# Whole x in two buffers, the multiple of 2 pi on another engine, joins in two pieces: one change in the Theta stage of a fused network

## The chip, the cores and the metric

The kernel runs on one core of a Trainium2 chip. The metric is the device time of one execution in microseconds; lower is better. The engines are TensorE (PE, matrix products), VectorE (DVE), ScalarE (ACT), GpSimd (POOL) and SyncE (SP), whose queue issues most of the DMA transfers.

## The reference, cut to what matters

Three blocks follow each other: an attention with sigmoid weights, a gated unit with a mixing over the sequence, and a block with phases. B is 4, the sequence 448, the width 768. The change lies in the third block:

```python
theta = x @ w_theta
zr, zi = x * np.cos(theta), x * np.sin(theta)
y = np.einsum('ts,bsd->btd', w_tok_r, zr) + np.einsum('ts,bsd->btd', w_tok_i, zi)
u = x + y
return u + np.maximum(u @ w_ch, 0.0)
```

## The kernel before

Every product in fp32 is made of three products of split operands: a high part (`acopy` on ScalarE, rounded to the matrix engine's format) and a low part (`sub` on VectorE, the rest), multiplied as high by high, high by low and low by high. The operand x lies in DRAM as `x_d[b]`, 768 by 448, feature by token.

**The Theta stage** works in units `(b, h, i)`: batch b, one half h of 384 features, one block i of 128 tokens. Blocks 0 to 2 are whole; the last 64 tokens of two batches make one block together, i = 3 of the even batch, so that there are 14 blocks (the list `steps`) and 28 units. `theta(b, h, i)` makes 18 matmuls of 384 columns (lines 636 to 638) into one of two PSUM banks `pt`, and then reduces the angle: line 641 forms round(theta / 2 pi) by adding and taking off (line 642) a large constant `MAGIC`; lines 643 and 644 take off the multiple of 2 pi in two parts; line 645 clamps. Line 643 is the last that reads the bank. ScalarE then forms Abs, Sin and the cosine as a Sin (lines 647 to 649), VectorE multiplies both by x^T (line 626), and `split` makes the two operands z of the token product. `tok(b, h, i, Z)` adds a unit's 18 matmuls of 448 columns (9 for a tail block) into six banks `py`, and at i = 3 VectorE adds x (line 59 through `add`) and y goes to DRAM. A list `queue` holds three units: `tok` of a unit is written down three units behind its `theta`.

**x is needed in three forms.** As the stationary operand `XT` of Theta, in blocks: `load_x2` loads a block `xf` from `x_d` (384 KB) and splits it, three blocks ahead. As x^T, token by feature, for the multiplications: `halve` transposes `x_d` by DMA as 16-bit halves into `halved`, `part_planes` sorts the two planes of a block by DMA into `xp`, and `join_planes` puts them together into `xr` with one ScalarE instruction of 1536 16-bit elements in each partition. And as the whole x for the addition at the end of a batch: `load_x` into the single buffer `xb`.

**Order.** In this stage only SP's queue keeps the order in which the program is written; the order of the other engines is laid out by a planner at build time, from the order of the program and from its own costs and due times, and each engine then works through its list in order. From batch 1 on `sums_ch` prepares blocks of w_ch alongside. Ahead of Theta lie the projections of the last batches (`project`, `ppo`); behind it the channel products of the last stage, whose first operands come from y in DRAM (`load_y`, `first_operands`).

Of the kernel before, what the change touches and what calls it, by code (L numbers as in the profile page):

```python
# [10 lines left out]
F32 = mybir.dt.float32  # L11
F32R = mybir.dt.float32r
# [10 lines left out]
P = 128  # L23
# [27 lines left out]
def net(ctx: ExitStack, tc: tile.TileContext, kq, vd, vl, w_in, w_sp, bsp, w_out, w_th, w_tok, w_ch, out):  # L51
# [3 lines left out]
    def sub(o, a, b):  # L55
        ve.tensor_tensor(out=o, in0=a, in1=b, op=ALU.subtract)  # L56
# [4 lines left out]
    def acopy(o, a, f=AF.Copy):  # L61
        se.activation(o, a, f)  # L62
# [416 lines left out]
    def halve(b):  # L479

        halved[b] = pxa.tile([P, 7, DM], U16, tag="xa", name="xa")
        nc.sync.dma_start_transpose(halved[b], x_d[b].bitcast(U16))
# [60 lines left out]
    es_a.close()  # L543


    pxb = es_w.enter_context(tc.tile_pool(name="pxb", bufs=1, reuse_waits="tile"))
    es_b = ExitStack()
    pb = es_b.enter_context(tc.tile_pool(name="pb", bufs=2, reuse_waits="tile"))
    pb.tile([P, LINE // 2], F32, name="gap2", bufs=1)
    XT, XR = {}, {}  # L550

    def load_x2(b, i):

        xf = pb.tile([P, KC, 2, LT], F32, tag="xf", name="xf")
        src = xf.rearrange("p c b t -> p c (b t)")
        if i < 3:
            nc.sync.dma_start(src, x_d[b][:, i * P:(i + 1) * P].rearrange("(c p) t -> p c t", p=P))
        else:
            for n in range(2):
                nc.sync.dma_start(xf[:, :, n, :], x_d[b + n][:, L0:S].rearrange("(c p) t -> p c t", p=P))  # L560
        t = pb.tile([P, KC, 2, P], F32R, tag="XT", name="XT", bufs=3)
        if not XT:
            pb.tile([P, LINE // 2], F32, name="gap3", bufs=1)
        acopy(t[:, :, 0, :], src)
        sub(t[:, :, 1, :], src, t[:, :, 0, :])
        XT[b, i] = t

    planes = {}
# [1 line left out]
    def part_planes(b, i):  # L570

        tail = i == 3
        n = b - b % 2 if tail else b
        if (n, i) not in planes:
            planes[n, i] = pb.tile([P, 2, DM], U16, tag="xp", name="xp")
        for j in (b % 2,) if tail else range(2):
            src = halved[b][:, 6 if tail else 2 * i + j, :]
            for h in range(2):
                nc.sync.dma_start(planes[n, i][halves[j], h, :], src[h:P:2, :])

    def join_planes(b, i):

        t = pb.tile([P, DM], F32, tag="xr", name="xr")
        acopy(t.bitcast(U16).rearrange("p (d h) -> p h d", h=2), planes[b, i])
        XR[b, i] = t

    def whole(pool, tag):
# [2 lines left out]
    def load_x(b):  # L590
        t = X2[b] = whole(pxb, "xb")
        nc.sync.dma_start(t, x_d[b].rearrange("(c p) t -> p c t", p=P))

    X2 = {}
    steps = [(b, i) for b in range(B) for i in range(4 - b % 2)]
    for n in steps[:2]:
        load_x2(*n)
        part_planes(*n)
    load_x2(*steps[2])
    join_planes(*steps[0])  # L600
    part_planes(*steps[2])
    se.activation(warm, XR[steps[0]][:, 0:4], AF.Sin, scale=0.0)
    for b, g in ((B - 2, G), (B - 1, Gn)):
        for d in range(KC):
# [23 lines left out]
    def theta(b, h, i):  # L628
        if (b, h, i) in LEFT:
            return [LEFT.pop((b, h, i))]  # L630
        hs = slice(h * HALF, (h + 1) * HALF)
        ps = ps_t.tile([P, 512], F32, tag="t", name="pt")
        o = ps[:, :HALF]
        t = XT[b, i]
        for k in range(KC):
            te.matmul(o, t[:, k, 0, :], thh[:, k, hs], start=k == 0, stop=False)  # L636
            te.matmul(o, t[:, k, 0, :], thl[:, k, hs], start=False, stop=False)  # L637
            te.matmul(o, t[:, k, 1, :], thh[:, k, hs], start=False, stop=k == KC - 1)  # L638
        r = pm.tile([P, HALF], F32, tag="r", name="r")
        m = pm.tile([P, HALF], F32, tag="m", name="m")  # L640
        ve.tensor_scalar(out=m, in0=o, scalar1=INV2PI, scalar2=MAGIC, op0=ALU.mult, op1=ALU.add)  # L641
        ve.tensor_scalar_sub(m, m, MAGIC)
        ve.scalar_tensor_tensor(out=r, in0=m, scalar=-C1, in1=o, op0=ALU.mult, op1=ALU.add)  # L643
        ve.scalar_tensor_tensor(out=r, in0=m, scalar=-C2, in1=r, op0=ALU.mult, op1=ALU.add)
        ve.tensor_scalar(out=r, in0=r, scalar1=PIN, scalar2=-PIN, op0=ALU.min, op1=ALU.max)  # L645
        x = XR[b, i][:, hs]
        se.activation(m, r, AF.Abs)  # L647
        se.activation(r, r, AF.Sin)
        se.activation(m, m, AF.Sin, bias=hpi, scale=-1.0)
        if i < 3:  # L650
            mul(m, x, m)
            mul(r, x, r)
            return [split(m, "zr"), split(r, "zi")]
        for n, a in enumerate((slice(0, 64), slice(64, P))):
            g = pz.tile([P, HALF], F32, tag="th", name="th", bufs=1)
            mul(g[0:64], x[a], m[a])
            mul(g[64:P], x[a], r[a])
            z = pz.tile([P, 2, HALF], F32R, tag="zl", name="zl", bufs=4)
            acopy(z[:, 0, :], g)
            sub(z[:, 1, :], g, z[:, 0, :])  # L660
            LEFT[b + n, h, i] = z
        return [LEFT.pop((b, h, i))]
# [5 lines left out]
    def tok(b, h, i, Z):  # L668
        if i == 0:
            for d in range(3):  # L670
                acc[h, d] = ps_y.tile([P, 512], F32, tag="y", name=f"py{d}")
        for d in range(3):
            ds = slice(d * P, (d + 1) * P)
            o = acc[h, d][:, :S]
            for n, z in enumerate(Z):
                c = 6 if i == 3 else 3 * n + i
                te.matmul(o, z[:, 0, ds], tkh[:, c, :], start=i == 0 and n == 0, stop=False)
                te.matmul(o, z[:, 0, ds], tkl[:, c, :], start=False, stop=False)
                te.matmul(o, z[:, 1, ds], tkh[:, c, :], start=False, stop=i == 3)
        if i == 3:  # L680
            for d in range(3):
                dc = 3 * h + d
                r = pz.tile([P, S], F32, tag="y", name="y", bufs=3)
                add(r, acc[h, d][:, :S], X2[b][:, dc, :])
                nc.sync.dma_start(y_d[b][dc * P:(dc + 1) * P, :], r)
# [41 lines left out]
    def sums_ch(n):  # L727

        if n % 3 == 0:
            c, s = quads[n // 3]  # L730
            q = pz.tile([P, 4, C2H], F32, tag="wq", name="wq", bufs=1)
            nc.sync.dma_start(q.rearrange("p (j i) f -> p j i f", j=2),
                              f_ch.rearrange("p (j c) (i f) -> p c j i f", j=2, i=2)[:, c, :, :, s])
            quad[:] = [q, c, s]
            return
        q, c, s = quad
        a11, a21, a12, a22 = (q[:, k] for k in range(4))
        if n % 3 == 1:
            for x, m in ((a11, "A11"), (a12, "A12")):
                half_part(x, m, c, s)  # L740
            for o, x, y, f in ((a22, a21, a22, ALU.add), (a21, a11, a21, ALU.subtract),
                               (a11, a22, a11, ALU.subtract), (a12, a12, a11, ALU.subtract)):
                nc.gpsimd.tensor_tensor(out=o, in0=x, in1=y, op=f)
        else:
            for x, m in ((a11, "S2"), (a22, "S1")):
                half_part(x, m, c, s)
            nc.sync.dma_start(f_s[:, c, :, s], q[:, 1:3])

    queue, done = [], []

    def unit(b, h, i):
        queue.append((b, h, i, theta(b, h, i)))
        if len(queue) > 3:
            tok(*queue.pop(0))
        if b >= CH_FROM and i < 3:
            sums_ch(len(done))
            done.append((b, h, i))

    with tc.manual_schedule(engines={mybir.EngineType.SP}):
        for b in range(B):  # L760
            for i in range(4):
                for h in range(2):
                    unit(b, h, i)
                    k = steps.index((b, i)) if (b, i) in steps else len(steps)
                    if h == 0:
                        if i == 1 and b % 2 == 0:
                            halve(b + 1)
                            part_planes(b + 1, 3)
                        if (b, i) == (1, 0):
                            halve(b + 1)  # L770
                        for n in steps[k + 1:k + 2]:
                            join_planes(*n)
                        for n in steps[k + 3:k + 4]:
                            part_planes(*n)
                        if i == 2:
                            load_x(b)
                    else:
                        for n in steps[k + 3:k + 4]:
                            load_x2(*n)
                        if (b, i) == (B - 1, 1):  # L780
                            Yf = {0: load_y(0, pxa)}
    es_m.close()
    es_th.close()
    py, p_t, p_y1 = (es_t.enter_context(tc.tile_pool(name=n, bufs=1, side="right", reuse_waits="tile"))
# [156 lines left out]
```

## Time and profile before

| | us |
|---|---|
| median of 3 runs (630.6 to 631.47) | 631.02 |
| the profiled execution | 629.19 |
| its span, first to last instruction | 627.4 |
| TensorE busy in it | 613.5 |
| VectorE busy | 426.4 |
| ScalarE busy | 334.7 |

The granted clock of TensorE was at its full level over the whole span. Times inside the execution count from the first instruction. A matmul's row shows its start and a modelled end; the rows of neighbours overlap, so what matters is the distance of their starts and the idle time in brackets, with the instruction that ended it.

### The profile page before, as it was taken

What the parts mean: (1) busy time and instruction counts of PE and PEld (TensorE: products, weight loads), DVE (VectorE), ACT (ScalarE), POOL (GpSimd) and SP (SyncE); (2) the same over time, 40 slices, a digit from 0 to 9 for tenths busy, and PEclk for the clock granted to TensorE, in tenths of its full rate; (3) what the DMA queues carried; (4) which work ended last, traced back from release to release, by engine and by line L of the source; (5) the groups of instructions that cost most, each with busy time, mean ns of one, the idle gap of its engine ahead of it and who ended that gap; (6) DMA issues with size and microseconds to landing.
All of it is one profiled execution on the core that took longest, in us unless ns stands there. A gap on an engine that the chain in (4) does not pass through costs nothing.

```text
span 627.4 us, 9178 instructions
## 1 busy us (share of the span) xinstructions
PE 613.5 (98%) x3296; PEld 506.9 (81%) x3296; DVE 426.4 (68%) x824; ACT 334.7 (53%) x544; POOL 24.3 (4%) x42
## 2 busy tenths in 40 slices
PE   7999999999999999999999999989999999999997
PEld 3456667756776689999999999979999989889896
DVE  3899566526754568884141677787797889679875
ACT  5798556553656335364264375455466466352540
POOL 0000000000001000100000000101001101000000
PEclk9999999999999999999999999999999999999999
DMA  8787588748864685865776416546368226344603
GB/s 319 244 272 208 194 270 261 254 155 287 284 210 152 183 280 193 256 207 177 193 217 174 105 50 217 111 152 201 100 153 245 70 91 225 115 167 132 242 31 133
DMA packets 95220, 118.13 MB, mean 188 GB/s; under 512 B 31171, under 2 KB 81733, under 8 KB 95173
## 3 DMA queue, kind: packets, MB, share of 16 engines
q1 hardware_dynamic: 87364, 104.69, 53.9%
q10 hardware_dynamic: 7808, 12.85, 5.6%
q8 instruction: 26, 0.43, 0.3%
q14 instruction: 22, 0.17, 0.1%
HBM read 73.57 MB, written 32.93 MB: 170 GB/s over the span
## 4 chain that ended last, share of the span: by engine, by line
PE 68%; DVE 17%; DMA 6%; ACT 6%; issue 2%; SPq 0%; ACTq 0%
PE psa L224 7%; PE pss L199 6%; PE psd L65 3%; PE psd L243 3%; DMA xf<-x_d 3%; PE ppo L66 3%; PE ppo L65 3%; PE ppo L67 3%; PE psd L67 3%; PE psd L66 3%; PE psd L244 3%; PE psd L245 3%; PE psp L450 2%; PE psp L449 2%; PE psp L451 2%
## 5 line engine op out<-in xcount | busy, mean ns | idle before, releaser
L186 ACT ACTIVATE af<-pss,bias 128x896 f32<-128x896 f32 x72 | 66.1, 1020 | 2.8 <-PE pss L199 2.8
L636 PE MATMUL pt<-thh,XT 128*128 128x384 f32 x168 | 57.2, 340 | 4.2 <-DVE r L643 4.2
L637 PE MATMUL pt<-thl,XT 128*128 128x384 f32 x168 | 56.8, 338 | 0.0
L224 PE MATMUL psa<-af,vr 128*64 128x448 f32 x288 | 56.8, 543 | 0.0
L638 PE MATMUL pt<-thh,XT 128*128 128x384 f32 x168 | 56.8, 338 | 0.0
L224 PEld LDWEIGHTS psa<-af,vr 128*64 128x64 f32 x288 | 19.6, 137 | 36.3 <-issue 35.4
L111 DVE SCALAR_TENSOR_TENSOR wq<-wraw,wq 128x384 int32<-128x384 int32 (+2 forms) x51 | 28.7, 594 | 24.1 <-ACT wraw L106 23.9
L62 ACT ACTIVATE ev<-psd 128x448 f32<-128x448 f32 (+1 forms) x30 | 17.0, 568 | 52.5 <-PE psd L67 23.2
L647 ACT ACTIVATE m<-r 128x384 f32<-128x384 f32 x28 | 14.6, 520 | 43.7 <-DVE r L645 43.7
L636 PEld LDWEIGHTS pt<-thh,XT 128*128 128x128 f32 x168 | 31.5, 188 | 5.9 <-DVE r L643 5.5
L65 PE MATMUL psd<-X,wih 128*128 128x448 f32 x96 | 35.6, 371 | 0.0
L106 ACT ACTIVATE wraw<-wraw 128x384 f32<-128x384 f32 (+2 forms) x51 | 29.7, 605 | 10.5 <-DVE wq L99 6.7
L66 PE MATMUL ppo<-g,wbh 128*128 128x448 f32 x96 | 35.2, 366 | 0.0
L65 PE MATMUL ppo<-g,wbh 128*128 128x448 f32 x96 | 35.1, 366 | 0.0
L67 PE MATMUL ppo<-g,wbl 128*128 128x448 f32 x96 | 35.1, 366 | 0.0
L67 PE MATMUL psd<-X,wil 128*128 128x448 f32 x96 | 35.1, 365 | 0.0
L66 PE MATMUL psd<-X,wih 128*128 128x448 f32 x96 | 35.1, 365 | 0.0
L56 DVE TENSOR_TENSOR X<-psa,X 128x448 fp32r<-128x448 f32 x24 | 15.0, 624 | 27.9 <-ACT X L62 27.9
L637 PEld LDWEIGHTS pt<-thl,XT 128*128 128x128 f32 x168 | 31.6, 188 | 0.4
L101 DVE SCALAR_TENSOR_TENSOR wq<-wraw,wq 128x384 int32<-128x384 int32 (+2 forms) x51 | 30.6, 600 | 1.8
L638 PEld LDWEIGHTS pt<-thh,XT 128*128 128x128 f32 x168 | 31.5, 188 | 0.0
L641 DVE TENSOR_SCALAR m<-pt 128x384 f32<-128x384 f32 x28 | 15.4, 551 | 19.6 <-DMA x_d<-x 17.9
(287 smaller groups left out, 1596.3 us busy)
## 6 DMA issues: line engine op xcount, KB each, us to landing
kqr<-in_kq SPq DMA_DIRECT2D x24, 448.0 KB, 4.8
wraw<-in_w_in SPq DMA_DIRECT2D x12, 512.0 KB, 5.6
x_d<-x ACTq DMA_DIRECT2D x24, 224.0 KB, 3.2
xp<-xa SPq DMA_DIRECT2D x56, 96.0 KB, 2.5
xb<-x_d SPq DMA_DIRECT2D x4, 1344.0 KB, 6.5
y_d<-y SPq DMA_DIRECT2D x24, 224.0 KB, 2.0
out_t<-o SPq DMA_DIRECT2D x24, 224.0 KB, 2.0
vr<-in_vd SPq DMA_DIRECT2D x24, 192.0 KB, 3.8
```

Source lines behind the costliest of these rows:

```text
L65: te.matmul(ps, wh, xh, start=first, stop=False)
L66: te.matmul(ps, wh, xl, start=False, stop=False)
L67: te.matmul(ps, wl, xh, start=False, stop=last)
L101: ve.scalar_tensor_tensor(out=self.q, in0=self.hi, scalar=-(2 ** 31), in1=self.q, op0=ALU.bitwise_and, op1=ALU.bitwise_or)
L106: se.activation(self.lo.bitcast(F32), self.hi.bitcast(F32), AF.Copy, scale=2.0 ** -112)
L111: ve.scalar_tensor_tensor(out=self.q, in0=self.lo, scalar=3, in1=self.q, op0=ALU.logical_shift_left, op1=ALU.bitwise_or)
L186: se.activation(af, ps[:, :, :S], AF.Sigmoid, bias=bias, scale=1.0 / math.sqrt(D))
L199: te.matmul(ps[:, j, :S], t[w][a, 0, c], t[x][a, 1, :], start=n == 0, stop=n == 2)
L224: te.matmul(ps[a, :S], t["v"][:, 2 * c + j, :], t["a"][c][:, j, :], start=False, stop=c == 2)
L636: te.matmul(o, t[:, k, 0, :], thh[:, k, hs], start=k == 0, stop=False)
L637: te.matmul(o, t[:, k, 0, :], thl[:, k, hs], start=False, stop=False)
L638: te.matmul(o, t[:, k, 1, :], thh[:, k, hs], start=False, stop=k == KC - 1)
```

## The change

Five things, in the code below. The blocks `xf` and `load_x2` go: `split_x` takes a block's high and low part out of the whole x in `X2[b]`, for which there are now two buffers, and `load_x` is called earlier (batch 0 before the stage, batch 1 in the first unit, batches 2 and 3 at block 1 of the batch ahead of them, behind the `tok` there). `XT` has two buffers in place of three and is split one block ahead. Line 641 becomes a ScalarE activation of the same arithmetic, and `r` and `m` have three buffers. `join_planes` makes two instructions of 768 elements. The calls in the loop over units stand in another order: splits, plane transfers and transposes ahead of a unit's `tok`, loads, joins and `sums_ch` behind it.

```diff
-    pxb = es_w.enter_context(tc.tile_pool(name="pxb", bufs=1, reuse_waits="tile"))
+    pxb = es_w.enter_context(tc.tile_pool(name="pxb", bufs=2, reuse_waits="tile"))
...
-    def load_x2(b, i):
-
-        xf = pb.tile([P, KC, 2, LT], F32, tag="xf", name="xf")
-        src = xf.rearrange("p c b t -> p c (b t)")
-        if i < 3:
-            nc.sync.dma_start(src, x_d[b][:, i * P:(i + 1) * P].rearrange("(c p) t -> p c t", p=P))
-        else:
-            for n in range(2):
-                nc.sync.dma_start(xf[:, :, n, :], x_d[b + n][:, L0:S].rearrange("(c p) t -> p c t", p=P))
-        t = pb.tile([P, KC, 2, P], F32R, tag="XT", name="XT", bufs=3)
+    def split_x(b, i):
+
+        t = pb.tile([P, KC, 2, P], F32R, tag="XT", name="XT")
...
-        acopy(t[:, :, 0, :], src)
-        sub(t[:, :, 1, :], src, t[:, :, 0, :])
+        if i < 3:
+            src = X2[b][:, :, i * P:(i + 1) * P]
+            acopy(t[:, :, 0, :], src)
+            sub(t[:, :, 1, :], src, t[:, :, 0, :])
+        else:
+            for n, a in enumerate(halves):
+                src = X2[b + n][:, :, L0:S]
+                acopy(t[:, :, 0, a], src)
+                sub(t[:, :, 1, a], src, t[:, :, 0, a])
         XT[b, i] = t
...
-        acopy(t.bitcast(U16).rearrange("p (d h) -> p h d", h=2), planes[b, i])
+        o = t.bitcast(U16).rearrange("p (d h) -> p h d", h=2)
+        for s in (slice(0, HALF), slice(HALF, DM)):
+            acopy(o[:, :, s], planes[b, i][:, :, s])
...
+    load_x(0)
     for n in steps[:2]:
-        load_x2(*n)
         part_planes(*n)
-    load_x2(*steps[2])
+    split_x(*steps[0])
     join_planes(*steps[0])
-    part_planes(*steps[2])
...
-        r = pm.tile([P, HALF], F32, tag="r", name="r")
-        m = pm.tile([P, HALF], F32, tag="m", name="m")
-        ve.tensor_scalar(out=m, in0=o, scalar1=INV2PI, scalar2=MAGIC, op0=ALU.mult, op1=ALU.add)
+        r = pm.tile([P, HALF], F32, tag="r", name="r", bufs=3)
+        m = pm.tile([P, HALF], F32, tag="m", name="m", bufs=3)
+        se.activation(m, o, AF.Copy, bias=MAGIC, scale=INV2PI)
...
-                    unit(b, h, i)
+                    z = theta(b, h, i)
                     k = steps.index((b, i)) if (b, i) in steps else len(steps)
                     if h == 0:
-                        if i == 1 and b % 2 == 0:
-                            halve(b + 1)
+                        for n in steps[k + 1:k + 2]:
+                            split_x(*n)
+                        for n in steps[k + 2:k + 3]:
+                            part_planes(*n)
+                    if (b % 2, i, h) in ((0, 1, 0), (1, 0, 1)) and b + 1 < B:
+                        halve(b + 1)
+                    queue.append((b, h, i, z))
+                    if len(queue) > 3:
+                        tok(*queue.pop(0))
+                    if h == 0:
+                        if (b, i) == (0, 0) or 0 < b < B - 1 and i == 1:
+                            load_x(b + 1)
+                    else:
+                        if b % 2 == 0 and i == 1:
                             part_planes(b + 1, 3)
-                        if (b, i) == (1, 0):
-                            halve(b + 1)
                         for n in steps[k + 1:k + 2]:
                             join_planes(*n)
-                        for n in steps[k + 3:k + 4]:
-                            part_planes(*n)
-                        if i == 2:
-                            load_x(b)
-                    else:
-                        for n in steps[k + 3:k + 4]:
-                            load_x2(*n)
-                        if (b, i) == (B - 1, 1):
-                            Yf = {0: load_y(0, pxa)}
+                    if b >= CH_FROM and i < 3:
+                        sums_ch(len(done))
+                        done.append((b, h, i))
+                    if (b, h, i) == (B - 1, 1, 1):
+                        Yf = {0: load_y(0, pxa)}
```

## Rows read from the trace of the kernel before

**Rows 1.** The page: busy time, share of the span and instructions of each engine.

```profile
PE 613.5 (98%) x3296; PEld 506.9 (81%) x3296; DVE 426.4 (68%) x824; ACT 334.7 (53%) x544; POOL 24.3 (4%) x42
```

**Rows 2.** Busy time in stretches of the Theta stage, TensorE, weight load, VectorE, ScalarE, GpSimd.

```profile
402.60:417.50 14.90, 12.30 (x65) 11.16 (x63) 11.67 (x26) 8.22 (x15) 1.18 (x2) 1.00 0.39 131
...
496.70:508.40 11.70, 10.15 (x55) 9.50 (x53) 9.10 (x20) 5.79 (x10) 0.00 (x0) 1.00 0.05 19
...
sum 197.50, PE 193.28 PEld 182.86 DVE 155.29 ACT 108.86 POOL 16.40; mean PE 38.66 PEld 36.57 DVE 31.06 ACT 21.77 POOL 3.28
```

**Rows 3.** Timeline of TensorE: start, duration, line, operands, [idle before, and what ended it].

```profile
402.58 0.34 PE L636 MATMUL pt<-thh,XT 128*128 128x384 f32 x1
...
408.04 0.44 PE L636 MATMUL pt<-thh,XT 128*128 128x384 f32 x1 [0.28 <-DVE r L643]
...
417.46 0.44 PE L636 MATMUL pt<-thh,XT 128*128 128x384 f32 x1 [2.32 <-DVE r L643]
...
476.10 0.34 PE L636 MATMUL pt<-thh,XT 128*128 128x384 f32 x1
...
508.41 0.44 PE L636 MATMUL pt<-thh,XT 128*128 128x384 f32 x1 [1.56 <-DVE r L643]
...
551.39 0.68 PE L833 MATMUL pb__5486<-Y,wch 128*128 128x448 f32 x2 [1.45 <-DVE y L59]
```

**Rows 4.** Timeline of VectorE.

```profile
400.70 0.55 DVE L643 SCALAR_TENSOR_TENSOR r<-m,pt 128x384 f32<-128x384 f32 x1
...
415.98 0.96 DVE L56 TENSOR_TENSOR XT<-xf,XT 128x768 fp32r<-128x768 f32 x1 [1.50 <-ACT XT L62]
...
504.66 0.56 DVE L626 TENSOR_TENSOR r<-xr,r 128x384 f32<-128x384 f32 x1 [2.07 <-ACT r L648]
...
543.24 1.70 DVE L56 TENSOR_TENSOR T<-yf,xa 128x448 f32<-128x448 f32 x3 [5.01 <-DMA yf<-y_d]
```

**Rows 5.** The chain of waits, 400 to 418 us: start, duration, what.

```profile
409.92 5.10 DMA xf<-x_d
...
415.10 0.85 ACT XT L62
...
416.85 0.56 DVE r L643
```

**Rows 6.** Timeline of ScalarE.

```profile
330.46 1.19 ACT L62 ACTIVATE g<-gf 128x448 fp32r<-128x448 f32 x2
...
502.32 1.94 ACT L62 ACTIVATE xr<-xp 128x1536 uint16<-128x1536 uint16 x1
```

**Rows 7.** VectorE's groups, 347 to 544 us: busy us, mean ns | idle before.

```profile
L641 DVE TENSOR_SCALAR m<-pt 128x384 f32<-128x384 f32 x28 | 15.4, 551 | 19.6 <-DMA x_d<-x 17.9 <-PE pt L638 1.7
...
L56 DVE TENSOR_TENSOR XT<-xf,XT 128x768 fp32r<-128x768 f32 x11 | 10.9, 992 | 8.5 <-ACT XT L62 8.5
```

**Rows 8.** ScalarE's groups, 347 to 544 us.

```profile
L62 ACT ACTIVATE xr<-xp 128x1536 uint16<-128x1536 uint16 x12 | 23.4, 1947 | 0.3 <-issue 0.3
...
L62 ACT ACTIVATE XT<-xf 128x768 fp32r<-128x768 f32 x11 | 9.2, 839 | 8.5 <-DMA xf<-x_d 8.5
```

**Rows 9.** Loads into xb: issues with KB and median landing; landing of all.

```profile
xb<-x_d SPq DMA_DIRECT2D x4, 1344.0 KB, 6.5
...
DMA to landing us min/median/max: 4.4/6.5/9.4
```

**Rows 10.** Timeline of SP's queue, the waits at its instructions included in their time.

```profile
317.64 0.39 SPq L557 DMA_DIRECT2D xf<-x_d  x1
...
456.22 5.41 SPq L685 DMA_DIRECT2D y_d<-y  x3
```

**Rows 11.** ScalarE's groups, 300 to 347 us: the eviction of a PSUM bank.

```profile
L62 ACT ACTIVATE x<-ppo 128x448 f32<-128x448 f32 x17 | 9.1, 540 | 13.8 <-PE ppo L67 8.3 <-PE psp L453 2.2 <-DMA x_d<-x 1.9
```

**Rows 12.** Waits of ScalarE, 347 to 544 us: us in total, times, longest.

```profile
ACT m L647 <- DVE r L645: 43.7, 20, 4.9
```

**Rows 13.** Waits of TensorE's weight load, whole span.

```profile
PEld pt L636 <- DVE r L643: 5.5, 4, 2.7
```

More of the change, by code (lines that the diff above doesn't have):

```diff
@@ L749, in net @@
     queue, done = [], []
[L751 to L757, printed above, removed]
     with tc.manual_schedule(engines={mybir.EngineType.SP}):
```

## The prediction, made before the change was run

> **What bounds the kernel.** I read the page first: TensorE is busy for 613.5 of 627.4 us [rows 1]. At most 13.9 us can come from anything but fewer matmuls, and the change removes no matmul. So the question is only where TensorE stands still, and whether the change touches those places. The busy time by stretches shows it for the Theta stage (346.8 to 544.3 us): 193.28 of 197.50 us, and the 4.2 us that are missing lie almost wholly in two short stretches, 2.60 us between 402.6 and 417.5 and 1.55 us between 496.7 and 508.4 [rows 2]. TensorE's own timeline then gives the three instructions that waited: 0.28, 2.32 and 1.56 us, together 4.16 us, each the first matmul of a Theta unit (L636), each released by L643 on VectorE [rows 3]. L643 is the last reader of a Theta bank in PSUM; there are two banks, so unit n+2 cannot begin before L643 of unit n has ended. Both places are where a batch ends: the token products of a tail block are 9 matmuls instead of 18, so Theta units follow each other faster, and six additions of x fall on VectorE there as well.
>
> Elsewhere the release is in time. Of the 26 hand-overs of a bank, four had no margin: these three and one more, where only the weight load waited [rows 13]. The closest of the other 22 is the one before unit 11: L643 starts at 400.70 and takes 0.55, the matmul comes at 402.58, so 1.3 us are left [rows 3, 4].
>
> Why L643 is late there was read in the chain of waits and on the two engines. The 2.32 us: a block load of x that was issued at 409.92 and took 5.10 us, then ScalarE's high part of XT, then VectorE's low part, and only then L643 at 416.85 [rows 5]; VectorE had been idle for 1.50 us before that low part at 415.98 [rows 4]. The 1.56 us: VectorE was idle for 2.07 us at 504.66, waiting for a Sin on ScalarE [rows 4], which at that moment was in a join of x^T, 1.94 us in one piece from 502.32 [rows 6].
>
> **The change, part by part.**
>
> *No block loads.* The load in rows 5 no longer exists. At that place the next block comes from an x already in SBUF. Without the low part of XT in front of it, L643 could have run when VectorE fell idle, 415.98 - 1.50 = 414.48, and ended at 415.03; TensorE was ready at 417.46 - 2.32 = 415.14. So this part alone pays the 2.32 us. The copies and subtractions of XT stay (ScalarE 839 ns, VectorE 992 ns each [rows 7, 8]), and for two tail blocks become two of each, off TensorE.
>
> What replaces the loads is four loads of a whole x, 1344 KB each, which the kernel made anyway, now earlier. Loads into that buffer took 4.4 to 9.4 us from issue to landing, 6.5 in the middle (two smaller loads of y are among them) [rows 9]. The first goes out where the first block load went, at 317.64 [rows 10], and must land before Theta at 346.8: 317.64 + 9.4 = 327.0, plus 839 ns and 992 ns, about 329; 17 us of cover, by the projections of the last batches. On ScalarE it stands ahead of the last splits of g at 330.46, which the last projection needs [rows 6]; if it landed some 3 us later still, TensorE would feel it. I take nothing. The second has no early user. The third and fourth wait on SP for the last addition of the batch whose buffer they take; the stores of y ahead of them wait for the same additions, so the queue loses nothing new. Behind them stand the x^T plane transfers and the loads for the sums of w_ch. The fourth is the narrow one: those stores left at 456.22 + 5.41 = 461.63 [rows 10], so landing is 466.0 to 471.0, the tail's two copies and two subtractions take about 2.3 us (the sum in rows 7 and 8 plus a second start), giving 468 to 473; its unit starts at 476.10 [rows 3], or 2.6 us earlier if the first two waits are gone, so 473.5. Zero is my value; the bound is 3 us of loss if other work stands in front.
>
> *The multiple of 2 pi on ScalarE.* 28 instructions of 551 ns leave VectorE (15.4 us) [rows 7]. The trace has no ScalarE pass over 384 columns of PSUM; the nearest is the eviction of 448 columns at 540 ns [rows 11], so 0.46 (by columns) to 0.54 us, and I take 0.52: 14.6 us more on ScalarE, which waited 43.7 us for the reduced angle alone in this stage [rows 12]. In a unit's own chain it is a swap, 0.55 against 0.52 us plus one more hand-over between engines. In VectorE's queue it is a relief of 0.55 us for each unit ahead of L643. That pays the 0.28 us. For the 1.56 us it removes the 0.55 us of the waiting unit and of the one before it. If VectorE's relief is no cover, because something else fills it, the 0.28 and half of the 1.56 stay.
>
> The Trainium skill ("ScalarE: Activation LUTs", Rules for kernel authors) speaks against this part: for add and mul it says to use VectorE and not ScalarE. By that rule the move would lengthen the chain by an unknown amount; by rows 7 and 11 the two engines take the same time for this pass, and the sum goes by the rows.
>
> *Joins in halves.* 1947 ns become two pieces [rows 8]; each is between half of that, 0.97 us, and half plus a start of some 0.1 us; I take 1.05, so about 2 us more on ScalarE over 14 joins, covered by the same idle time. A Sin that waits behind a join can go between the halves: of the 2.07 us at 504.66 about 1 us goes. With the 1.1 us above this covers 1.56. If the halves stay together, 0.5 to 1.0 us of this wait stays.
>
> *The other order.* Halving x^T, plane transfers and joins move by up to one unit (7 us), with the same number of transfers; the split of a block runs one block ahead, not three. A unit and its block have at least one whole unit between them. I cost these at nothing; their cover is the same queue of three units.
>
> *Sum.* The profiled execution took 629.19 us (span 627.4 and 1.8 around it). 629.19 - 4.16 = 625.03. The median of the runs shown is 631.02, 1.83 above it; so the forecast is 625.03 + 1.83 = **626.9 us**.
>
> **Rivals.**
>
> *The gain stays partly behind the fourth load.* If the split of the tail block is queued behind other ScalarE work, TensorE waits about 2 us at the unit of 476 us: 628.9. For it: the margin of 0 to 5 us above. Against it: the additions come earlier too, with VectorE relieved.
>
> *The gain is given back at the hand-over to the last stage.* After Theta, VectorE stood 5.01 us at 543.24 for y from DRAM, its additions followed, and TensorE waited 1.45 us for them at 551.39 [rows 3, 4]. If that load of y comes no earlier while TensorE does, the 1.45 us become 5.6 and the time is 631.0. For it: a load sets its own pace. Against it: its issue follows the last unit's work on w_ch, which moves with TensorE. From the other side, VectorE has less to do there, so the 1.45 us may go as well: 625.4.
>
> *Slower: the multiple of 2 pi is late.* ScalarE works in order. If the pass over PSUM is placed behind the Abs of the unit before, it waits with it, 43.7 us in 20 waits, 2.2 us on average, up to 4.9 [rows 12], and L643 waits for it. Against the 0.55 us of relief that is 1.65 us net at each of the three places without margin: 631.0 + 5.0 = 636.0. From a net delay of 0.42 us at each (3 x 0.42 = 1.26, 0.2%) the kernel is slower. For it: ScalarE's waits are many, and releasing the bank then takes two engines. Against it: ScalarE waits because VectorE is behind, and VectorE gets shorter; outside the four, L643's margin is 1.3 us and more. The skill's rule above would read as this rival.
>
> **How the numbers follow.** All three waits gone or nearly so: 0.63, own range 625.0 to 628.2 (below, the 1.45 us and some tenths; above, 1 us left of the last wait and small change). Partly behind the load, 628.9: 0.08. Given back, or the freed time filled by other work, 631.0: 0.13. Slower, 636: 0.16. Faster by more than 0.2% (1.26 us, about what a measurement of this kernel tells from no change) is then 0.71, within it 0.13, slower 0.16. The range of 8 in 10 reaches over the first three cases to 632.3, where slower begins, and down to 624.8, leaving out 0.16 above and some 0.03 below.
>
> **What would show it.** Right: L636 waits for L643 nowhere for more than a few tenths; TensorE's idle time in the Theta stage falls from 4.2 us to under 1; VectorE's busy time falls by about 15 us and ScalarE's rises by 16 to 17; no wait of ScalarE for an x load behind 470 us; the wait at the start of the last stage is 1.5 us or less. Wrong: L636 waiting where the first pass of ScalarE stands behind an Abs or a join; a Theta unit or the last projection waiting for XT or g because a whole x landed late; the last stage's wait grown to 5 us.

## The result, and the profile after

The changed kernel takes 626.36 us (median of 8 runs, 624.9 to 628.32) against 631.94 us for the kernel before (8 runs beside it); the ratio is 0.9902, interval 0.9878 to 0.9926. The forecast was 626.9. The profiled execution took 626.07 us, its span is 624.3. From the first Theta matmul to the last instruction the two profiles show 627.4 - 346.8 = 280.6 and 624.3 - 347.9 = 276.4 us: 4.2 us less, where the sum said 4.16. The two numbers do not count quite the same, as the account below says. (The span differs by only 3.1, because ahead of the change, at the start of the kernel, TensorE happened to wait 1.5 us for a load that cost it 0.3 before.)

The line numbers of the kernel after are shifted by one and two: Theta's matmuls are lines 637 to 639, the pass over PSUM 642, the releasing instruction 644. The busy time by stretches, columns as in [rows 2]:

```profile
402.60:417.50 14.90, 14.90 (x81) 14.37 (x80) 13.92 (x32) 9.85 (x20) 0.00 (x0) 1.00 0.45 145
...
494.40:505.40 11.00, 10.71 (x58) 10.04 (x57) 8.73 (x19) 7.79 (x16) 1.20 (x2) 1.00 0.01 3
...
sum 193.30, PE 192.62 PEld 183.16 DVE 145.36 ACT 121.03 POOL 15.91; mean PE 38.52 PEld 36.63 DVE 29.07 ACT 24.21 POOL 3.18
```

In the first stretch TensorE now never stands still, in the second for 0.29 us; over the stage 0.68 us are missing instead of 4.2 (the other 0.39 us is a wait for an operand z at 533.56). TensorE's timeline at the same places, to hold against [rows 3]:

```profile
415.41 0.34 PE L637 MATMUL pt<-thh,XT 128*128 128x384 f32 x1
...
504.96 0.44 PE L637 MATMUL pt<-thh,XT 128*128 128x384 f32 x1 [0.29 <-DVE r L644]
...
544.46 0.48 PE L832 MATMUL pa__5430<-Y,wch 128*128 128x448 f32 x1 [1.27 <-DVE y L59]
...
548.73 0.47 PE L832 MATMUL pb__5474<-Y,wch 128*128 128x448 f32 x1 [0.35 <-DVE y L59]
```

The 2.32 us and the 0.28 us are gone, of 1.56 us 0.29 are left, and the hand-over to the last stage costs 1.62 us in two waits instead of 1.45 in one. Of the two engines' groups in the stage, those that are new:

```profile
L642 ACT ACTIVATE m<-pt 128x384 f32<-128x384 f32 x28 | 13.3, 474 | 5.9 <-PE pt L639 5.9
...
L62 ACT ACTIVATE xr<-xp 128x768 uint16<-128x768 uint16 x24 | 24.4, 1066 | 0.0
...
L648 ACT ACTIVATE m<-r 128x384 f32<-128x384 f32 x28 | 14.6, 520 | 32.5 <-DVE r L646 32.5
```

The pass costs 474 ns on ScalarE (estimate 520), half a join 1066 ns (estimate 1050), and ScalarE's wait for the reduced angle fell from 43.7 [rows 12] to 32.5 us. Over the whole span VectorE's busy time fell by 10.6 us, not 15 (426.4 to 415.8), and ScalarE's rose by 12.2, not 16: two of the forecast's signs came out smaller. A part of this is that the rows of neighbours overlap. In the kernel before, line 641 at 505.14 takes 0.55 us by its row, but the next instruction starts at 505.60; in a full queue the pass takes 0.46 us and not 0.55.

### The profile page after: what moved, and what is told of

It is laid out like the page before. It is cut to its first block, busy times and chain, and to the rows that moved or that the text cites. A ratio compares the mean times of both kernels' runs of the same rounds, so it can differ in the third digit from the quotient of the medians.

```text
span 624.3 us, 9178 instructions
## 1 busy us (share of the span) xinstructions
PE 612.6 (98%) x3296; PEld 507.1 (81%) x3296; DVE 415.8 (67%) x798; ACT 346.9 (56%) x588; POOL 23.8 (4%) x42
## 4 chain that ended last, share of the span: by engine, by line
PE 79%; DVE 11%; DMA 4%; ACT 3%; issue 2%; SPq 0%; POOL 0%; ACTq 0%; POOLq 0%; DVEq 0%
PE psa L224 7%; PE pss L199 6%; PE psd L65 3%; PE psd L243 3%; PE ppo L66 3%; PE ppo L67 3%; PE ppo L65 3%; PE psd L66 3%; PE psd L67 3%; PE psd L245 3%; PE psd L244 3%; PE pt L638 3%; PE pt L639 3%; PE pt L637 3%; PE py L678 3%; PE py L679 3%
## 5 line engine op out<-in xcount | busy, mean ns | idle before, releaser
L648 ACT ACTIVATE m<-r 128x384 f32<-128x384 f32 x28 | 14.6, 520 | 32.5 <-DVE r L646 32.5
L62 ACT ACTIVATE xr<-xp 128x768 uint16<-128x768 uint16 x28 | 28.4, 1066 | 0.5 <-ACT x L62 0.5
```

## The experiments

Ratios are to the kernel before, run beside each on the same chip.

**The kernel before, again.** No edit.

> The kernel before, unchanged, as a second profile of it. The first profile shows 4.2 us of waits in the Theta stage, the profile of the changed kernel 0.7, a difference of 3.5 us, while the medians differ by 5.6. Theory: the three waits (0.28, 2.32, 1.56 us) stand in every execution at the same instructions and are the whole change; then this profile shows 4.2 us again within 0.5, and the rest of the 5.6 is spread between executions outside the stage. Rival: the first profile was a short one, and this one shows 6 to 7 us of waits in the Theta stage or right behind it.

Measured: 632.14 us, ratio 0.9975 (0.9952 to 0.9998): so far apart can a kernel stand from itself. The profile, span 631.2, shows the wait of 2.27 us at the same instruction, 1.44 us at the third, and something that the first profile did not have. The stretch behind the first wait, microsecond by microsecond (the third number from the right is the granted clock as a share of full speed):

```profile
417.00:418.00 1.00, 0.64 (x4) 0.23 (x2) 0.00 (x0) 0.44 (x1) 0.79 (x2) 1.00 0.90 341
418.00:419.00 1.00, 0.00 (x0) 0.00 (x0) 0.57 (x1) 1.00 (x2) 0.00 (x0) 1.00 0.02 7
419.00:420.00 1.00, 0.09 (x1) 0.09 (x1) 1.00 (x3) 1.00 (x1) 0.00 (x0) 1.00 0.00 0
420.00:421.00 1.00, 1.00 (x4) 1.00 (x5) 1.00 (x3) 0.22 (x1) 0.00 (x0) 0.52 0.00 0
421.00:422.00 1.00, 1.00 (x5) 1.00 (x4) 0.97 (x4) 0.38 (x1) 0.00 (x0) 0.50 0.74 259
422.00:423.00 1.00, 1.00 (x5) 1.00 (x4) 0.96 (x3) 0.97 (x3) 0.00 (x0) 0.50 0.81 266
423.00:424.00 1.00, 1.00 (x6) 1.00 (x5) 1.00 (x4) 0.21 (x1) 0.00 (x0) 0.77 0.52 186
424.00:425.00 1.00, 1.00 (x8) 0.99 (x7) 0.68 (x2) 0.99 (x3) 0.00 (x0) 1.00 0.31 109
```

TensorE stood still, and when it went on its clock fell to the lower of its two levels (0.50 is 1.2 of 2.4 GHz): the counts of matmuls in a microsecond go from 7 or 8 down to 4 to 6. The four rows lose 0.48 + 0.50 + 0.50 + 0.23 = 1.71 us. So this wait cost 2.27 us and then 1.71 again. In the first profile of before the same wait had no such tail, which is one reason why that execution, at 629.19, was shorter than nearly all others. Of the 12 executions of this run 6 had a mean clock under 0.998; they took 632.87 us on average, the other 6 took 630.98. Of 86 executions of the kernel before that the other experiments were held against, 44 had it, 633.6 us against 631.45 on average; but they come from three chips, on which 21 of 28, 9 of 33 and 14 of 25 had it, and within a chip the difference is 1.0 to 3.4 us. Of the 8 of the changed kernel none had it; of the 8 of the kernel before beside them the clock is not on record.

**The join in one piece again.**

```diff
-        o = t.bitcast(U16).rearrange("p (d h) -> p h d", h=2)
-        for s in (slice(0, HALF), slice(HALF, DM)):
-            acopy(o[:, :, s], planes[b, i][:, :, s])
+        acopy(t.bitcast(U16).rearrange("p (d h) -> p h d", h=2), planes[b, i])
```

> The changed kernel with the join of x^T in one instruction again. The forecast gave the halves about 1 us at the wait of 1.56 us, by a Sin that goes between them. In the trace of the changed kernel the two halves stand back to back everywhere, so the theory now is: no difference, 626.4 within 0.6 us, and the remaining 0.3 us wait of TensorE for line 644 unchanged. Rival (the forecast's own): the whole join holds Sin up again, a wait of about 1.3 us comes back at the end of batch 2, 627.4.

Measured: 625.9 us, ratio 0.9893 (0.9855 to 0.9932), the same as with halves; the profile, span 621.6, has no wait for a bank at all. The halves pay nothing. The reason stands in ScalarE's timeline of the changed kernel at the place that the forecast had in mind:

```profile
497.13 1.99 ACT L62 ACTIVATE xr<-xp 128x768 uint16<-128x768 uint16 x2
```

The planner put the halves back to back here, ahead of the unit's Abs (499.49), and no Sin goes between them. The expectation above is wrong in one point: the halves do not stand back to back everywhere. Three of the stage's joins are apart (from 381.60, 469.47 and 480.25), but none with a Sin in between.

**The multiple of 2 pi on VectorE again.**

```diff
-        se.activation(m, o, AF.Copy, bias=MAGIC, scale=INV2PI)
+        ve.tensor_scalar(out=m, in0=o, scalar1=INV2PI, scalar2=MAGIC, op0=ALU.mult, op1=ALU.add)
```

> The changed kernel with the multiple of 2 pi on VectorE again (line 642 as line 641 was). Theory, relief of VectorE: 0.55 us in each unit falls back on its queue, the bank is released later at the ends of the batches, and 0.3 to 1.9 us of waits for the bank come back there: 626.7 to 628.3. Rival, chain: an engine change less in each unit releases the bank earlier, the remaining 0.3 us wait goes, 626.1. Third: none of both matters with whole x loads, 626.4.

Measured: 631.67 us, ratio 0.9979 (0.9956 to 1.0002): nearly all of the gain is gone, more than was expected. Waits of TensorE in total, times, longest, and the stretch behind:

```profile
PE pt L637 <- DVE r L644: 2.3, 1, 2.3
```

```profile
505.00:510.00 5.00, 2.71 (x15) 2.21 (x13) 4.82 (x10) 3.13 (x8) 1.28 (x2) 0.97 0.00 0
510.00:515.00 5.00, 5.00 (x20) 4.99 (x21) 5.00 (x11) 2.53 (x6) 0.00 (x0) 0.69 0.39 141
```

The wait at the end of batch 2 is back, longer than before, and the clock falls behind it: the two stretches lose 1.7 us by it. In 9 of 12 executions the mean clock was under 0.998. Those 9 took 631.70 us on average and the other 3 took 631.57, so in the times of this kernel the fall of the clock does not show.

**Both of these: only the whole x and the new order are left.** Its edit is the two diffs above together.

> The changed kernel with VectorE forming the multiple and with the join in one piece: what is left of the change is the whole x in two buffers and the new order of calls. By the forecast's sum this part alone pays the 2.32 us wait and nothing else: waits of 0.3 and 1.6 us stay, about 628.5. Rival: the stage had only one cause, the late block loads, and all waits go: 626.4. Rival on the other side: the loads were not the cause, the 2.32 us stays: 630.

Measured: 629.35 us, ratio 0.9952 (0.9926 to 0.9978). The places of the old 2.32 us and 0.28 us waits are free. Left are 0.98 us for a bank at the end of batch 2 (506.35) and 1.39 us for an operand z near the end of the stage (535.94). TensorE's waits:

```profile
PE py L676 <- ACT zr L62: 1.4, 1, 1.4
PE pt L635 <- DVE r L642: 1.0, 1, 1.0
```

So the whole x and the order pay about 3 us, and ScalarE's pass on top of it 0.9952 to 0.9893, some 3.7 us; these two intervals overlap at their ends. The same kernel with halves stands at 0.9979, where the whole x and the order would pay only 1.3 us; those two intervals overlap as well, and the planner laid the two kernels out differently.

**ScalarE's pass alone, in the kernel before.**

```diff
-        ve.tensor_scalar(out=m, in0=o, scalar1=INV2PI, scalar2=MAGIC, op0=ALU.mult, op1=ALU.add)
+        se.activation(m, o, AF.Copy, bias=MAGIC, scale=INV2PI)
```

> The kernel before, block loads and all, with line 641 alone moved to ScalarE. Theory: VectorE's queue loses 0.55 us in each unit, so the waits of 0.28 and 1.56 us go, while the 2.32 us wait for the late block load stays, and with it the fall of TensorE's clock that followed such a wait in two other profiles (3.5 us at the lower level, some 1.7 us): ratio about 0.997. Rival: ScalarE's pass comes late behind an Abs and the bank is released later, ratio 1.00 to 1.008. Second rival: the relief reaches the 2.32 us wait too, ratio 0.992.

Measured: 630.99 us, ratio 0.9994 (0.9964 to 1.0024): no gain that can be told. In its profile the 1.56 us wait is gone, as expected, the 0.28 us has become 0.49 and the 2.32 us has become 1.44. At that last place VectorE did not stand still for the block load any more: it worked without a break from 412.40 to the release at 417.45, the split at 416.29 included. TensorE's waits:

```profile
PE pt L636 <- DVE r L643: 1.9, 2, 1.4
PE pa__5442 L833 <- DVE y L59: 1.5, 1, 1.5
PE pb__5486 L833 <- DVE y L59: 0.4, 1, 0.4
```

That execution took 628.48 us, the other 11 all more; 5 of 12 had a fallen clock.

**One block load earlier, in the kernel before.**

```diff
         queue.append((b, h, i, theta(b, h, i)))
+        k = steps.index((b, i)) if (b, i) in steps else len(steps)
+        if h == 1:
+            for n in steps[k + 3:k + 4]:
+                load_x2(*n)
         if len(queue) > 3:
...
-                        for n in steps[k + 3:k + 4]:
-                            load_x2(*n)
```

> The kernel before with one call moved: load_x2 of a block stands ahead of the token products of its unit and so ahead of the stores of y in SP's queue. Theory: the 2.32 us wait is the block load held up in SP's queue by the stores of the batch's y; it goes, and with it the fall of the clock; waits of 0.28 and 1.4 to 1.6 us stay: ratio 0.993 to 0.996. Rival: the load is early, but the split of its block still stands ahead of the release in VectorE's queue; a wait of 0.5 to 1 us stays there, 0.997. Second rival: the wait came from VectorE's load alone, ratio 1.0.

Measured: 634.98 us, ratio 1.0038 (1.0003 to 1.0073), slower. The edit does not single out the load, for the planner laid the stage out anew, with a wait of 3.72 us at the end of batch 2 and the clock low behind it. But the place of the 2.32 us can be read. The load now stood ahead of the stores of y in SP's queue and left at 409.06; counted from the first Theta matmul (348.93, in the kernel before 346.79) that is 3.0 us earlier. VectorE still waited 1.24 us for the split at 413.70, then worked for 4.5 us without a break before the release at 419.16, and TensorE waited 1.12 us there. TensorE's waits (us in total, times, longest) and the stretch behind the longest:

```profile
PE pt L636 <- DVE r L643: 6.3, 4, 3.7
```

```profile
515.00:520.00 5.00, 5.00 (x17) 5.00 (x16) 5.00 (x12) 3.02 (x8) 0.00 (x0) 0.50 0.39 141
```

So the earlier load went along with a shorter wait at its own place, and what was left there was VectorE's queue, as the first rival has it; the time was lost elsewhere. What an early load by itself is worth in time stays open; what the block loads cost rests on the kernels without them.

**VectorE's old pass kept as dead work.** The line added writes r, which line 644 overwrites.

```diff
+        ve.tensor_scalar(out=r, in0=o, scalar1=INV2PI, scalar2=MAGIC, op0=ALU.mult, op1=ALU.add)
         se.activation(m, o, AF.Copy, bias=MAGIC, scale=INV2PI)
```

> The changed kernel, with the old pass over the bank kept on VectorE as well, its result written into r and overwritten by line 644: ScalarE still forms the multiple, VectorE has its 0.55 us for each unit back as dead work. Theory, relief of VectorE's queue: the waits at the ends of the batches come back as with the multiple on VectorE (0.9979 of before), ratio 0.996 to 0.999. Rival, the shorter or other chain through ScalarE matters and not the queue: ratio stays 0.990.

Measured: 631.17 us, ratio 0.9978 (0.9949 to 1.0008), the same as with the multiple on VectorE (0.9979), though ScalarE forms it. So what pays in the move to ScalarE is what VectorE's queue loses in each unit. One doubt stays: the planner laid out this kernel anew too, and its waits are other than those with the multiple on VectorE, 0.42, 1.51 and 3.47 us at the end of batch 2 where that kernel has one of 2.29. TensorE's waits for a bank:

```profile
PE pt L637 <- DVE r L645: 5.4, 3, 3.5
```

**Abs done twice: 0.52 us more on ScalarE.**

```diff
         se.activation(m, r, AF.Abs)
+        se.activation(m, r, AF.Abs)
```

> The changed kernel with the Abs of each unit done twice: 0.52 us more on ScalarE in each unit, between the clamp and the Sin. It tests how near ScalarE is to the rival that the multiple of 2 pi comes late. Theory: ScalarE's waits for the clamp (32.5 us) cover it and only the wait of 0.3 us grows to 0.5 to 1.5 us: ratio 0.991 to 0.994. Rival: ScalarE is now as near the limit as VectorE was; the waits at the ends of the batches come back with a fall of the clock, ratio 0.997 or more. Third: no effect, 0.990.

Measured: 632.5 us, ratio 0.9994 (0.9969 to 1.002): the whole gain lost, though ScalarE has 32.5 us of waits for the clamp alone. VectorE's wait for the Sin at the end of batch 2, first in the changed kernel and then here:

```profile
493.22 0.55 DVE L627 TENSOR_TENSOR th<-xr,r 64x384 f32<-64x384 f32 x1 [1.15 <-ACT r L649]
```

```profile
499.76 0.55 DVE L627 TENSOR_TENSOR th<-xr,r 64x384 f32<-64x384 f32 x1 [1.70 <-ACT r L650]
```

The Abs stands between VectorE's clamp and VectorE's product, so VectorE stands still longer by just the added time, and at the end of the batch TensorE waits 0.67 and 1.90 us for a bank, with the clock low from 512 to 515 (0.71 on average from 510 to 515). That the one follows from the other by way of VectorE's queue is read from the order of the rows; no run holds the planner's order fixed. (In this execution TensorE also waited 2.0 us at 298, ahead of Theta, for ScalarE's eviction of a projection, and the clock fell there too. Such a wait of 0 to 2.1 us comes and goes from execution to execution and from kernel to kernel.)

**Halves alone, in the kernel before.** The edit is that of the changed kernel.

> The kernel before with the joins in two halves and nothing else. Theory, from the changed kernel, where the halves stand back to back: nothing, ratio 1.000 within 0.003. Rival, the forecast's: the Sin of unit 24 goes between the halves and the 1.56 us wait falls by about 1 us, ratio 0.998. Second rival: the planner's new order moves a wait of 1 to 3 us somewhere else, ratio 1.003 to 1.008, as the one earlier load call did.

Measured: 631.8 us, ratio 0.9994 (0.9969 to 1.0019): no gain that can be told, though 0.998 is not excluded. The profile shows the forecast's own mechanism at work. At the end of batch 2 the Sin (line 650) and the cosine (651) stand between the halves, and VectorE's wait for that Sin is 1.18 us where it was 2.07 in both profiles of the kernel before:

```profile
503.91 1.07 ACT L62 ACTIVATE xr<-xp 128x768 uint16<-128x768 uint16 x1
504.84 0.50 ACT L650 ACTIVATE r<-r 128x384 f32<-128x384 f32 x1
505.24 0.60 ACT L651 ACTIVATE m<-m,hpi 128x384 f32<-128x384 f32 x1
505.75 1.07 ACT L62 ACTIVATE xr<-xp 128x768 uint16<-128x768 uint16 x1
...
505.37 0.56 DVE L628 TENSOR_TENSOR r<-xr,r 128x384 f32<-128x384 f32 x1 [1.18 <-ACT r L650]
```

From that product (line 628) to the release VectorE's list is the same as in the kernel before, instruction by instruction, and TensorE's wait there is 0.65 us where it was 1.56 and 1.44. The other large wait is 1.61 for 2.32 and 2.27, in another order of VectorE's list.

**The calls behind the token products, as the kernel before had its own.** `tok` and `sums_ch` stand ahead of splits, plane transfers and transposes.

```diff
-                    z = theta(b, h, i)
+                    queue.append((b, h, i, theta(b, h, i)))
+                    if len(queue) > 3:
+                        tok(*queue.pop(0))
+                    if b >= CH_FROM and i < 3:
+                        sums_ch(len(done))
+                        done.append((b, h, i))
...
-                    queue.append((b, h, i, z))
-                    if len(queue) > 3:
-                        tok(*queue.pop(0))
...
-                    if b >= CH_FROM and i < 3:
-                        sums_ch(len(done))
-                        done.append((b, h, i))
```

> The changed kernel with splits, plane transfers and transposes behind the token products and the sums of w_ch of a unit, where the kernel before had its own. Theory: the new order of calls pays nothing by itself; ratio 0.990 within 0.003. Rival: the order matters, since the releases stand behind other work at the ends of the batches; waits of 1 us and more come back there, ratio 0.993 to 0.998.

Measured: 628.3 us, ratio 0.9921 (0.9895 to 0.9947); this does not separate it from 0.9902. In TensorE's waits stands the one rival of the forecast that is about the loads:

```profile
PE pt L637 <- ACT XT L62: 1.5, 1, 1.5
```

It is the unit of the second tail block, at 480.50 us. The split of the last whole x came 1.48 us late, because the x itself did. In SP's queue a transpose of `halve` now stands between the stores of y and this load, which left at 472.50 where the changed kernel's left at 460.39, and ScalarE stood waiting for it:

```profile
479.93 0.52 ACT L62 ACTIVATE XT<-xb 128x384 fp32r<-128x384 f32 x1 [4.05 <-DMA xb<-x_d]
```

**The hand-over, first try.** The differences T are written down behind the last `tok`, in the changed kernel with whole joins.

```diff
-    first = first_operands(0)
+    first = [operand(y) for y in Yf[0]]
     while queue:
         tok(*queue.pop(0))
+    first = first_operands(0, *first)
```

> The changed kernel with whole joins, and the differences T of the last stage written down behind the last token products, where the additions of x to y then stand ahead of them. What is left of waits at the hand-over is 1.1 and 0.3 us of TensorE for those additions. Theory: they go, 1.0 to 1.4 us less than whole joins alone (ratio about 0.987). Rival: the differences come later and TensorE waits for them or for S2's operands instead, ratio 0.989 to 0.992.

Measured: 626.8 us, ratio 0.9924 (0.9892 to 0.9956): nothing gained. VectorE's list still had T (from 540.16) ahead of the additions (from 544.09); TensorE still waited 0.9 and 0.4 us.

**The hand-over, second try.** T is bound behind the additions, whose instructions `tok` now keeps in `adds`.

```diff
-        T1 = both(sub, y1[0], y0[0])
-        return B11, B21, T1, both(sub, y1[1], T1)
+        with tc.issue_after(adds[B - 1, 2].ins):
+            T1 = both(sub, y1[0], y0[0])
+        with tc.issue_after(adds[B - 1, 5].ins):
+            T2 = both(sub, y1[1], T1)
+        return B11, B21, T1, T2
```

> The changed kernel with whole joins, and the differences T of the last stage bound behind the additions of x to the last y: T1 behind those of the first half, T2 behind those of the second. Writing them down later had left the order of VectorE as it was. Theory: the 1.1 and 0.3 us that TensorE waits at the hand-over for these additions go, 1.2 us less than whole joins alone, ratio 0.987 to 0.988. Rival: T and its operands come later and TensorE waits for them in the second or third product, ratio 0.989 to 0.992.

Measured: 625.51 us, ratio 0.9875 (0.9843 to 0.9908), the best of the study. All that TensorE waits for between 340 and 560 us in its profile is one line:

```profile
PE py L678 <- ACT zr L62: 0.4, 1, 0.4
```

The two waits of the hand-over are gone. From the first Theta matmul to the end of the span the profile takes 624.4 - 350.6 = 273.8 us against 621.6 - 346.6 = 275.0 with whole joins alone, the 1.2 us of the expectation; but the times do not separate it from whole joins alone (0.9893).

## Why the prediction came out right, step by step

**The reading of the bound held.** TensorE's three waits were nearly all that this stage had to give, and from the first Theta matmul on the profile is 4.2 us shorter, as summed. That the two agree so closely is in part luck. TensorE's idle time in the stage fell by 3.5 us and not 4.16 (0.29 us are left, and 0.39 for an operand z are new), and the hand-over took 0.17 us more; the other 0.8 us are not idle time in the rows. One piece of it is that the matmuls right behind a wait start further apart: 0.28 us, at 417.46 and 417.74, where 0.17 is usual. The measured gain is larger: 0.98% of 632 us, 6.2 us, with 4.7 at the lower end of the interval. Held against the second profile of the kernel before, the same stretch is 631.2 - 348.6 = 282.6 us for 276.4, also 6.2 us, and 1.7 of that is the fall of the clock, which was not in the sum. As an estimate, half of the executions of before losing 1.7 to 2.15 us by it makes about 1 us on average; the changed kernel lost none. Some 1 us is left that no run here settles; executions of one kernel differ by 2 us either way, and the waits ahead of Theta differ between them.

**No block loads: the 2.32 us.** Right in what it paid: with whole x and the new order alone that place has no wait, nor has that of the 0.28 us, which the forecast gave to the other part; ratio 0.9952, some 3 us (0.9979 with halves). That the lateness of the load was the whole cause is argued from the chain of waits and not shown. Two profiles speak for a share of VectorE's queue: with the load 3.0 us earlier 1.12 us are left at this place, and with ScalarE's pass alone, where VectorE no longer stood still for the load, 1.44 us. Both are in other orders of VectorE's list.

**The multiple of 2 pi.** The mechanism, relief of VectorE's queue, is shown by the dead work, within what an order laid out anew leaves open: 0.9978 with it, 0.9902 without, and the intervals are apart. The size was put too low: 0.28 us and 1.1 of the 1.56 in the forecast; measured are 3.7 us with whole joins (0.9952 to 0.9893, intervals that overlap) and 4.9 with halves (0.9979 to 0.9902). Without the pass, at the place of the 1.56 us, TensorE waits 0.98 us in the one profile (and 1.39 us for an operand z later on), and 2.29 us in the other with 1.7 us of fallen clock behind it. The forecast had no term for the later wait nor for the clock; what remains of the 3.7 and 4.9 us no run settles. Alone the part shows no gain in time, 0.9994 (0.9964 to 1.0024), though in its profile TensorE's waits from Theta to the hand-over are 3.8 us for 5.6. The rule of the Trainium skill that was weighed there ("ScalarE: Activation LUTs", Rules for kernel authors: add and mul on VectorE) would have cost most of the gain here (0.9979); 474 ns on ScalarE stand against 551 on VectorE, and the queue decides.

**The joins in halves.** This step failed in the changed kernel. The forecast gave the halves 1 us of the third wait. In the changed kernel the join at that place stands ahead of the unit's Abs, not between the Abs and the Sin, so there was no Sin to let through; with and without halves the time is the same (0.9902 and 0.9893), and the third wait went by the relief of VectorE. That the total came out all the same is luck in this term. The mechanism itself is real: in the kernel before, where the Sin does stand behind the join, halves took 0.89 us off VectorE's wait for it (2.07 to 1.18) and some 0.8 to 0.9 off TensorE's, though the time of the whole kernel does not show it.

**ScalarE's idle time as cover.** Right for the pass over PSUM, wrong as a rule. Half a microsecond more of ScalarE inside the chain from clamp to product takes the whole gain back (0.9994). ScalarE's waits for the clamp are time in which VectorE has its turn at the unit, and in these runs they covered the pass and the joins but not an instruction between the clamp and the product. Slower than the kernel before, as the third rival has it, no kernel with the change was.

**The rivals.** The fourth load did not hold the tail block up in this order: ScalarE waited 0.85 us for it at 468.12, VectorE's part of the split ended at 469.24, and the unit began at 473.92, so 4.7 us were left. In the old order of the calls it did, by 1.48 us where 2 were put. The order, which the forecast put at nothing, thus sets when this load leaves, though the times of the two orders are not apart. The hand-over gave nothing back: 1.62 us for 1.45.

## What to carry to other kernels

When TensorE waits for the release of a bank, read what stands ahead of the releasing instruction in its engine's queue, with every wait in it, and take work from that queue; in these runs it mattered less where the work went than whether it lay in the chain that the queue waits for. Price a wait of TensorE with the clock behind it: here two microseconds of standing still often cost nearly four. And where a planner lays out the engines' lists, look in the built list whether an edit that is to open a gap (a cut in two, a later call) has moved anything, before trusting it with a share of the gain.

## What was not expected of the hardware

The clock. It was at its full level all over the two profiles compared in the result, yet in the Theta stage it fell to the lower one behind waits of TensorE of 1.9 us (Abs twice), 2.27 (before, again), 2.3 (multiple on VectorE), 3.5 (dead work) and 3.7 us (early load), and ahead of it behind waits of 2.0 and 2.1 us (Abs twice, calls behind the products). It stayed up behind the 2.32 us in the first profile of before and behind the waits up to 1.6 us in this stage. In the case laid out above it took 1.71 us, in the others about 1.7 each, and 3.4 behind the 3.7 us. ScalarE's pass over 384 columns of PSUM, 474 ns, is a little cheaper than its passes over SBUF of the same width, 509 to 523.
